# S5 and SwiGLU in parallel on one core: the second x chunk and the parameters on GpSimd's DMA queue, the first weights back to back on SyncE's

## The chip, the core, the metric

The kernel runs on one core of one Trainium2 chip. The metric is device time in microseconds, the median of several executions. Every execution also has a span, from its first to its last instruction; the time is 1.7 to 2.4 us longer than the span.

## The reference

The input x is [2048, 512] in bfloat16. It is normalized (LayerNorm), and two branches read the result: a diagonal complex state space (S5) and a gated feed-forward (SwiGLU). Their sum and x are the output.

```python
xn = _layernorm(x)
# branch A: B_bar from Lambda, log_dt, B;  h_t = Lam_bar * h_(t-1) + B_bar xn_t;  y = 2 Re(C h) + xn * Dskip
# branch B: (silu(xn @ w1) * (xn @ w3)) @ w2        w1, w3: [512, 1792], w2: [1792, 512]
return x + A(xn) + B(xn)
```

## The kernel before

The tokens go in four blocks of four chunks of 128 rows. TensorE is the bottleneck from the first block's gate matmuls on. The change touches only the start, which looks like this (cuts marked with `# ...`). SyncE (`nc.sync`), ScalarE (`nc.scalar`) and GpSimd (`nc.gpsimd`) can issue DMAs.

```python
def load_w(f0, f1, eng1=nc.sync, eng3=nc.sync):       # gate tiles of 128 columns: tile f is f*P .. (f+1)*P
    eng1.dma_start(out=w1_sb[:, :, f0:f1], in_=w1v[:, :, f0:f1])
    eng3.dma_start(out=w3_sb[:, :, f0:f1], in_=w3v[:, :, f0:f1])

for c in range(2):                                     # chunks 0 and 1, each in two halves on two queues
    for eng, dsl in ((nc.sync, slice(0, D // 2)), (nc.scalar, slice(D // 2, D))):
        eng.dma_start(out=x_blk[0][:, c, dsl], in_=xv[:, c, dsl])
nc.scalar.dma_start(out=x_blk[0][:, 3, :], in_=xv[:, 3, :])
nc.sync.dma_start(out=x_blk[0][:, 2, :], in_=xv[:, 2, :])
load_w(0, 2 * P)
for i, src in enumerate((A_log_dt, A_Lambda_re, A_Lambda_im)):     # the parameters, 1 KB each
    nc.sync.dma_start(out=par_rows[i * NPT:(i + 1) * NPT, :], in_=src.rearrange("(t p) -> t p", p=P))
load_w(2 * P, 4 * P)
# ... later loads of x blocks 1, 2, 3 on nc.sync, each as one DMA: load_x(1), load_x(2), load_x(3)

keep_busy(NWARM, TBLK)                                 # NWARM = 10 warm-up matmuls on TensorE
# ...
ln_stats(0, 0)              # VectorE, program order: statistics of chunk 0,
ln_first_rstd(0)            # (ScalarE)
bulk_loads()
ln_stats(0, 1)              # then of chunk 1,
ln_first_rstd(1)
ln_first_transpose(0, 2)    # and only then the normalization of chunk 0, which TensorE transposes
keep_busy(4, P)
ln_apply(0, 1)
ln_first_transpose(1)
# ... statistics and normalization of chunks 2 and 3
quarter(0, (0, 1), 2)       # TensorE: chunk 0 times gate tiles 0 and 1 (w1, then w3)
pps = params_transpose()    # TensorE transposes the parameters; ScalarE and GpSimd go on with them
params_dt(pps)
params_turn()
table_angles(0)             # VectorE, from the parameters
table_angles(1)
quarter(1, (0, 1))
ln_first_transpose(2)
quarter(0, (2,))            # chunk 0 times gate tile 2
ln_first_transpose(3)
# ...
```

## Time and profile before

| | |
|---|---|
| time | 204.51 us, median of 3 (204.32 to 204.80) |
| span of the profiled execution | 203.1 us |
| TensorE busy | 198.3 us (98%) |
| end of TensorE's part of the chain that ended last | 198.87 us (its very last matmul ends at 200.08) |

The view of waits of the kernel before, for TensorE alone, has two lines: who waited for whom, the sum in us, how often, the longest. The second is the launch; the first is the only time in 203 us that TensorE waited for data.

```profile
PE bu_ps L557 <- DMA w_sb<-in_B_w_dram: 1.0, 1, 1.0
PE bu_ps L193 <- PEq L883: 0.8, 1, 0.8
```

The timeline of the kernel before, TensorE alone: start, duration, engine, line of the kernel, operation, output and input, count, and in brackets the idle time before it with what ended it. L193 is the warm-up, L238 the transposes of x, L557 the quarters, L525 the full gate matmuls.

```profile
0.76 4.43 PE L193 MATMUL bu_ps<-const-bfloat16-1.0 128*128 128x512 bf16 x10 [0.76 <-PEq L883]
5.10 0.65 PE L238 MATMUL y_ps<-ident,xn 128*128 128x128 bf16 x4
...
8.49 0.39 PE L557 MATMUL bu_ps<-xnT,w_sb 128*128 128x128 bf16 x4
9.89 0.40 PE L557 MATMUL bu_ps<-xnT,w_sb 128*128 128x128 bf16 x4 [1.01 <-DMA w_sb<-in_B_w_dram]
...
13.47 8.80 PE L525 MATMUL gu_ps<-xnT,w_sb 128*128 128x512 bf16 x40
```

TensorE comes out of its warm-up at 5.19 us straight into the transposes. At 8.49 us it multiplies with the w1 half of gate tile 2; the w3 half is not there until 9.89. The view of the chain that ended last says the same: a DMA of weights, and from 9.89 us on TensorE without a hole.

```profile
4.71 5.13 DMA w_sb<-in_B_w_dram
9.85 0.05 issue
9.89 0.40 PE bu_ps L557 x4
```

And VectorE, in the timeline of all engines, waits for chunk 1 (the second of the statistics), but only for 0.17 us:

```profile
2.82 0.69 DVE L214 BATCH_NORM_STATS2 stats<-x_blk 128x6 f32<-128x512 bf16 x1 [2.82 <-DMA x_blk<-in_A_x_dram]
3.90 0.69 DVE L214 BATCH_NORM_STATS2 stats<-x_blk 128x6 f32<-128x512 bf16 x1 [0.17 <-DMA x_blk<-in_A_x_dram]
```

The trace also records when each of the 16 DMA engines signs off a transfer. "First..last" below is the first and the last of the 16.

```
kernel before, profiled execution       issued   landed, first..last engine
x chunk 1, two halves                    1.16    2.89..3.69 and 3.12..3.88
gate tiles 0/1, w1 and w3           2.11, 2.59   5.11..5.47 and 5.90..6.48
gate tiles 2/3, w1                       4.27    6.80..7.79
gate tiles 2/3, w3                       4.71    7.60..9.85
```

### The profile page before, as it was taken

What the parts mean: (1) busy time and instruction counts of PE and PEld (TensorE: products, weight loads), DVE (VectorE), ACT (ScalarE), POOL (GpSimd) and SP (SyncE); (2) the same over time, 40 slices, a digit from 0 to 9 for tenths busy, and PEclk for the clock granted to TensorE, in tenths of its full rate; (3) what the DMA queues carried; (4) which work ended last, traced back from release to release, by engine and by line L of the source; (5) the groups of instructions that cost most, each with busy time, mean ns of one, the idle gap of its engine ahead of it and who ended that gap; (6) DMA issues with size and microseconds to landing.
All of it is one profiled execution on the core that took longest, in us unless ns stands there. A gap on an engine that the chain in (4) does not pass through costs nothing.

```text
span 203.1 us, 3444 instructions
## 1 busy us (share of the span) xinstructions
PE 198.3 (98%) x1317; PEld 122.8 (60%) x1317; DVE 172.7 (85%) x242; ACT 125.4 (62%) x251; POOL 39.0 (19%) x65
## 2 busy tenths in 40 slices
PE   8899999999999999999999999999999999999994
PEld 2784444444444488854444445888444458888993
DVE  3779699999999999989949999999999935584832
ACT  4699897699999977959766676110566662101010
POOL 3250269700310143021111010310101110000000
PEclk9999999999999999999999999999999999999999
DMA  6899999992573042926796004466330780101011
GB/s 173 248 247 191 312 203 106 350 281 42 101 146 66 0 90 57 183 86 118 68 194 131 13 13 94 91 143 132 90 65 0 149 162 2 52 3 52 29 40 39
DMA packets 28696, 23.16 MB, mean 114 GB/s; under 512 B 16008, under 2 KB 26376, under 8 KB 28680
## 3 DMA queue, kind: packets, MB, share of 16 engines
q1 hardware_dynamic: 25512, 13.21, 27.9%
q0 software_dynamic: 2592, 9.44, 24.9%
q10 hardware_dynamic: 576, 0.30, 0.5%
q8 instruction: 10, 0.16, 0.3%
q14 instruction: 6, 0.05, 0.1%
HBM read 7.74 MB, written 2.10 MB: 48 GB/s over the span
## 4 chain that ended last, share of the span: by engine, by line
PE 93%; DMA 3%; SPq 2%; DVE 1%; issue 0%
PE gu_ps L525 45%; PE gu_ps L724 16%; PE y_ps L724 9%; PE bu_ps L724 7%; PE bu_ps L435 7%; PE y_ps L435 7%; DMA w_sb<-in_B_w_dram 3%; PE gu_ps L557 1%; PE bu_ps L557 1%; DVE xn L735 1%; SPq L166 0%; SPq L151 0%; SPq L161 0%; SPq L152 0%; DVE x_blk L735 0%
## 5 line engine op out<-in xcount | busy, mean ns | idle before, releaser
L525 PE MATMUL gu_ps<-xnT,w_sb 128*128 128x512 bf16 x424 | 92.5, 379 | 0.0
L525 PEld LDWEIGHTS <-w_sb 128*128 128x128 bf16 x424 | 41.4, 98 | 49.4
L724 PEld LDWEIGHTS <-act 128*128 128x128 f16 x451 | 43.2, 98 | 5.5
L534 ACT ACTIVATE g<-gu_ps 128x512 bf16<-128x512 f32 x55 | 33.1, 602 | 14.6 <-PE gu_ps L525 14.4
L535 ACT ACTIVATE u<-gu_ps 128x512 bf16<-128x512 f32 x55 | 33.2, 603 | 9.8 <-PE gu_ps L525 9.5
L543 DVE TENSOR_TENSOR act<-g,u 128x1024 f16<-128x1024 bf16 x28 | 19.0, 677 | 4.4 <-ACT u L535 4.4
L435 PEld LDWEIGHTS <-bt 128*128 128x128 bf16 x128 | 12.5, 98 | 15.1
L478 DVE TENSOR_TENSOR_SCAN u<-rho,act,u 128x512 bf16<-128x512 f32 x16 | 19.6, 1266 | 0.0
L492 POOL DMA_DIRECT2D act<-p x8 | 7.2, 900 | 45.8 <-DVE act L488 31.8
L435 PE MATMUL bu_ps<-xnT,bt 128*128 128x512 bf16 x64 | 15.1, 379 | 0.0
L435 PE MATMUL y_ps<-xnT,bt 128*128 128x512 bf16 x64 | 15.1, 379 | 0.0
L457 DVE TENSOR_TENSOR p<-u,tabe 128x2048 bf16<-128x2048 bf16 x8 | 9.8, 1219 | 2.6 <-DMA act<-p 2.5
L724 PE MATMUL y_ps<-tw,act 128*128 128x256 f16 x88 | 10.9, 272 | 0.0
L437 ACT ACTIVATE u<-y_ps 128x512 bf16<-128x512 f32 x16 | 9.5, 595 | 2.3 <-PE y_ps L435 2.1
L724 PE MATMUL gu_ps<-w_sb,act 128*128 128x256 bf16 (+1 forms) x84 | 10.8, 268 | 0.0
L724 PE MATMUL gu_ps<-tw,act 128*128 128x256 f16 x88 | 10.7, 273 | 0.0
L437 ACT ACTIVATE u<-bu_ps 128x512 bf16<-128x512 f32 x16 | 9.5, 595 | 2.0 <-PE bu_ps L435 1.9
L468 POOL DMA_DIRECT2D u<-p x6 | 5.3, 878 | 26.8 <-ACT u L535 7.9
L744 ACT ACTIVATE bu_ps<-y_ps 128x256 f32<-128x256 f32 x4 | 1.5, 369 | 13.7 <-PE y_ps L724 13.7
L461 DVE TENSOR_TENSOR u<-u,tabe 128x2048 bf16<-128x2048 bf16 x8 | 9.8, 1220 | 0.2
L478 DVE TENSOR_TENSOR_SCAN u<-rho,ends,u 128x512 bf16<-128x512 f32 x8 | 9.9, 1268 | 0.0
L484 DVE TENSOR_TENSOR p<-u,tabe 128x2048 f16<-128x2048 bf16 x8 | 9.8, 1221 | 0.1
(143 smaller groups left out, 275.1 us busy)
## 6 DMA issues: line engine op xcount, KB each, us to landing
act<-p POOLq DMA_DIRECT2D x8, 512.0 KB, 4.7
u<-p POOLq DMA_DIRECT2D x6, 512.0 KB, 4.7
xn<-x_blk POOLq DMA_DIRECT2D x4, 512.0 KB, 5.6
out_dram<-xn SPq DMA_DIRECT2D x15, 128.0 KB, 1.7
w_sb<-in_B_w_dram SPq DMA_DIRECT2D x1, 1792.0 KB
x_blk<-in_A_x_dram SPq DMA_DIRECT2D x3, 512.0 KB, 9.0
w_sb<-in_B_w_dram SPq DMA_DIRECT2D x2, 768.0 KB, 7.1
w_sb<-in_B_w_dram SPq DMA_DIRECT2D x4, 256.0 KB, 3.7
```

The source lines that it names most:

```text
L435: nc.tensor.matmul(out=ps, lhsT=bt[:, ri, dt, pt * P:(pt + 1) * P], rhs=xnT_blk[b][:, dt, :], start=(dt == 0), stop=(dt == NDT - 1))
L437: nc.scalar.activation(out=u[:, j, ri, :], in_=ps, func=ACT.Copy)
L457: nc.vector.tensor_tensor(out=st["p"][:, :, ::-1, :], in0=st["g"], in1=tabe[:, psl, 2:0:-1, :], op=ALU.mult)
L461: nc.vector.tensor_tensor(out=st["g"], in0=st["g"], in1=tabe[:, psl, 0:1, :].to_broadcast(FULL), op=ALU.mult)
L478: nc.vector.tensor_tensor_scan(out=v, data0=rho[:, pt:pt + 1].to_broadcast([P, TBLK]), data1=v, initial=init, op0=ALU.mult, op1=ALU.add)
L484: nc.vector.tensor_tensor(out=st["p16"][:, :, ::-1, :], in0=st["g"], in1=tabe[:, psl, 1:3, :], op=ALU.mult)
L492: gp.dma_start(out=act_state(b, hf), in_=st["p16"], accum_op=ALU.add)
L525: nc.tensor.matmul(out=ps[:, tsl], lhsT=w[:, dt, f * P:(f + 1) * P], rhs=xnT[:, dt, tsl], start=(dt == 0), stop=(dt == NDT - 1))
L534: nc.scalar.activation(out=g16[:, f % 2, :], in_=g_ps, func=ACT.Silu)
L535: nc.scalar.activation(out=u16[:, f % 2, :], in_=u_ps, func=ACT.Copy)
L543: nc.vector.tensor_tensor(out=act(b)[:, k0:k1 + 1:k1 - k0, :], in0=g16, in1=u16, op=ALU.mult)
L724: nc.tensor.matmul(out=out, lhsT=left[:, k, :], rhs=right[k][:, cols], start=(start and k == 0), stop=(k == NK - 1), skip_group_check=True)
```

## The change

The intent: take everything out of SyncE's queue that stands ahead of the weights of gate tiles 2 and 3, so that they are issued some 1.6 us earlier and TensorE's one stall goes. (Landing is the moment at which a transfer's data are in and its semaphore has been counted up.) Chunk 1 and the parameters go to GpSimd's queue; the parameters' transpose moves behind the next quarter; and later loads of x are split.

```diff
-    for c in range(2):
-        for eng, dsl in ((nc.sync, slice(0, D // 2)), (nc.scalar, slice(D // 2, D))):
-            eng.dma_start(out=x_blk[0][:, c, dsl], in_=xv[:, c, dsl])
+    nc.gpsimd.dma_start(out=x_blk[0][:, 1, :], in_=xv[:, 1, :])
+    for eng, dsl in ((nc.sync, slice(0, D // 2)), (nc.scalar, slice(D // 2, D))):
+        eng.dma_start(out=x_blk[0][:, 0, dsl], in_=xv[:, 0, dsl])
     # ... chunks 3 and 2
     load_w(0, 2 * P)
-    for i, src in enumerate((A_log_dt, A_Lambda_re, A_Lambda_im)):
-        nc.sync.dma_start(out=par_rows[...], in_=...)
     load_w(2 * P, 4 * P)
     # ...
-        load_x(1)
+        load_x(1, 2)
     # ...
-        load_x(2)
-        load_x(3)
+        load_x(2, 4)
+        load_x(3, 2)
     # ... after the memset and affine_select of ident on GpSimd
+    for i, src in enumerate((A_log_dt, A_Lambda_re, A_Lambda_im)):
+        nc.gpsimd.dma_start(out=par_rows[...], in_=...)
     # ...
             quarter(0, (0, 1), 2)
+            quarter(1, (0, 1))
             pps = params_transpose()
     # ... params_dt, params_turn, table_angles(0), table_angles(1)
-            quarter(1, (0, 1))
             ln_first_transpose(2)
```

More of the change, by code (lines that the diff above doesn't have):

```diff
@@ L164 @@
     load_w(0, 2 * P)
-    for i, src in enumerate((A_log_dt, A_Lambda_re, A_Lambda_im)):
-        nc.sync.dma_start(out=par_rows[i * NPT:(i + 1) * NPT, :], in_=src.rearrange("(t p) -> t p", p=P))
     load_w(2 * P, 4 * P)
@@ L200 @@
                             base=0, pattern=[[-1, P]], channel_multiplier=1)
+    for i, src in enumerate((A_log_dt, A_Lambda_re, A_Lambda_im)):
+        nc.gpsimd.dma_start(out=par_rows[i * NPT:(i + 1) * NPT, :], in_=src.rearrange("(t p) -> t p", p=P))
     nc.gpsimd.iota(iota_i, pattern=[[1, TBLK]], base=1, channel_multiplier=0)
```

## The prediction

> **What bounds the kernel now.** TensorE: busy 198.3 of 203.1 us (page, part 1). The chain of waits runs through TensorE without a gap from 9.89 us to 198.87 us. So only the start can move the total. TensorE's only data stall there is at 9.89: the third gate tile's first w3 matmul waited 1.0 us (the waits view says 1.01) for the w3 columns of tiles 2 and 3. In the landing records that load was issued at 4.71 and landed engine by engine from 7.60 to 9.85; its w1 twin was issued at 4.27 and landed at 7.79. Before the stall, TensorE is dense from 5.10 (it comes out of its warm-up matmuls, which end at 5.19) to 8.88.
>
> **What the change removes, adds, moves.**
> - SyncE issues at 0.40 to 0.51 us each. The three parameter issues (0.44, 0.26, 0.29) and one half-chunk issue (0.41) leave its queue ahead of the weights. Tiles 2 and 3 should be issued near 2.6 and 3.1 instead of 4.27 and 4.71.
> - The parameters' packets leave the weights' rings. The DMA rate per 25 ns shows a trough at 5.55 to 6.2 us (some 300 GB/s down to 130) just where they pass, and the spread of the 16 engines' landings grows after it: 0.6 us (tile 0/1 w3), 1.0, 2.25 (the stalled load).
> - Bytes are unchanged: 1.57 MB of x and tile 0 to 3 weights. The Trainium skill ("DMA: Bandwidth & Descriptors", Issuing engines are not separate DMA queues) says another issuing engine saves only issue time; the trace agrees in that DMA runs near 300 GB/s whenever fed. From a first packet at 1.75, an estimate with those 300 GB/s puts the stalled load's landing at 7.6 to 8.6, before TensorE wants it (8.66 after its w1 half).
> - x chunk 1 comes over GpSimd. Later GpSimd DMAs took 0.86 us to issue and 0.57 us more to the first packet; from 0.72 that makes landing about 3.2 to 3.9 against 3.88 now. VectorE's second statistics (3.90, ahead of the first normalization) wait for it.
> - GpSimd's three parameter issues (some 0.9 us each) put its iota and cast 2.7 to 3.6 us later, finished near 6.5, wanted at 9.1: free. Parameters land near 7, and their transpose now stands behind quarter 1: no TensorE wait. VectorE's angle tables start about 0.6 us later (9.7), still done before the first gate product.
> - Split loads of x blocks 1 to 3: seven issues instead of three, off the chain.
>
> **On the critical path.** Up to 1.0 us, the whole stall, if chunk 1 is not later than today. ScalarE's table load (11.26) follows TensorE and moves along. VectorE is full from 25 to 82 us and moves only some 0.6 us, but the tightest operand I see (the s4 difference, done 75.46, read 76.46) has 1.0 us of slack. I count 0.8 us.
>
> **Prediction: 203.7 us, 80% range 203.0 to 205.0.** Faster by over 2%: 0.01; within 2%: 0.98; slower: 0.01.
>
> **Right if** the waits view shows no TensorE wait on weights (or under 0.3 us), the chain becomes dense from about 5.1 us, the first tile-3 matmul group (13.64 now) starts near 12.7, and everything later keeps that offset.
>
> **Wrong if** GpSimd's first DMA has a cold start: the first one in this trace sent its first packet 3.74 us after its issue ended, all later ones within 0.8. VectorE was in long bf16 products then, so the cause is open (the skill, "SBUF — State Buffer", The "DVE blocks DMA" trap, would fit; at 0.7 us VectorE is idle). With it chunk 1 lands near 6, normalization slips 2 us and the result is about 205.5. Also wrong if the straggling DMA engines stay 2 us behind without the parameters, or if VectorE's smaller shift makes TensorE wait near 76 us.

## The result, and the profile after

| | before | after |
|---|---|---|
| time, median of 4 | 204.43 us (204.32 to 204.80) | 204.29 us (204.16 to 204.34) |
| ratio | | 0.9989, 95% interval 0.9972 to 1.0006: the same |
| span of the profiled execution | 203.1 us | 202.4 us |

Ratios are the mean time of one kernel's fast runs over that of the other's in the same rounds, so they are not quite the ratio of the medians.

The two profiles differ by 0.7 us, the times by 0.14 us. That is the first thing to notice: the profile before was taken in an execution (204.89 us) longer than each of the four that were timed.

The view of waits of the kernel after, TensorE alone. The wait for weights is gone and a wait for VectorE's normalization is new:

```profile
PE bu_ps L191 <- PEq L883: 0.8, 1, 0.8
PE y_ps L238 <- DVE xn L219: 0.6, 1, 0.6
```

The timeline of the kernel after, TensorE alone. The first transposes stand at 5.80 instead of 5.10 us; there is no gap at gate tile 2 (x8 at 9.04), and the full gate matmuls start 0.63 us earlier than in the profile before (12.84 for 13.47).

```profile
5.80 0.54 PE L238 MATMUL y_ps<-ident,xn 128*128 128x128 bf16 x4 [0.61 <-DVE xn L219]
...
8.81 0.40 PE L238 MATMUL y_ps<-ident,xn 128*128 128x128 bf16 x4
9.04 0.61 PE L557 MATMUL bu_ps<-xnT,w_sb 128*128 128x128 bf16 x8
```

Those full matmuls, and chunk 1's path, are in the timeline of all engines: GpSimd's DMA instruction starts at 1.27 us, VectorE's second statistics wait 0.73 us for the chunk and start at 4.60 instead of 3.90.

```profile
1.27 0.74 POOL L159 DMA_DIRECT2D x_blk<-in_A_x_dram  x1 [0.84 <-POOLq L883]
...
4.60 0.69 DVE L214 BATCH_NORM_STATS2 stats<-x_blk 128x6 f32<-128x512 bf16 x1 [0.73 <-DMA x_blk<-in_A_x_dram]
...
12.84 3.40 PE L525 MATMUL gu_ps<-xnT,w_sb 128*128 128x512 bf16 x14
```

The chain that ended last, kernel after, now begins with chunk 1 instead of the weights, 3.31 us from GpSimd's issue to the landing:

```profile
1.27 3.31 DMA x_blk<-in_A_x_dram
4.58 0.02 issue
4.60 0.70 DVE stats L214
```

The landing records:

```
kernel after, profiled execution        issued   landed, first..last engine
x chunk 2 / chunk 3 (SyncE, ScalarE) 1.18, 1.16  3.19..3.79 / 3.38..3.97
x chunk 1 (GpSimd; first packet 3.12)    1.27    3.94..4.58
gate tiles 0/1, w1 and w3           1.64, 2.11   4.80..5.71 and 5.72..6.57
gate tiles 2/3, w1                       2.67    6.60..7.46
gate tiles 2/3, w3                       3.21    7.47..8.32
```

So the weights did what was hoped, 9.85 to 8.32 us, and chunk 1 took part of it back. The stall cost 1.19 us in that profile: the eight matmuls of gate tile 2 began at 8.49 and ended at 10.29, and without a gap they take 0.61 us, as in the kernel after, and would have ended at 9.10. (The expectations below count 1.35 us.) The late chunk 1 put the first transposes 0.70 us back; at gate tile 2 TensorE is still 0.55 us behind (9.04 for 8.49). That leaves 0.64 us, which is about the difference of the two profiles. Three questions remain: why the times do not show those 0.65 us, what chunk 1 costs, and what the split loads do.

### The profile page after: what moved, and what is told of

Read it like the earlier page. It is cut to its first block, busy times and chain, and to the rows that moved or that the text cites. A ratio compares the mean times of both kernels' runs of the same rounds, so it can differ in the third digit from the quotient of the medians.

```text
span 202.4 us, 3438 instructions
## 1 busy us (share of the span) xinstructions
PE 197.4 (98%) x1304; PEld 122.5 (61%) x1317; DVE 172.5 (85%) x242; ACT 125.1 (62%) x251; POOL 44.7 (22%) x69
## 4 chain that ended last, share of the span: by engine, by line
PE 95%; DMA 2%; DVE 1%; issue 1%; POOLq 0%
PE gu_ps L525 45%; PE gu_ps L724 16%; PE y_ps L724 9%; PE bu_ps L724 7%; PE y_ps L435 7%; PE bu_ps L435 7%; PE gu_ps L557 2%; DMA x_blk<-in_A_x_dram 2%; PE bu_ps L557 1%; PE y_ps L238 1%; DVE xn L735 1%; DVE stats L214 0%; DVE x_blk L735 0%; DVE xn L219 0%; PE bu_ps L191 0%
```

## The experiments

Twelve runs on three chips, four on each, every one with five timed rounds beside the kernel before on the same chip. The table has spans of all executions (us): lowest, median, highest. The chips are numbered here as they come up; on which chip the first result was taken is not on record here.

```
chip  run              lowest  median  highest   before there: lowest, median, highest   ratio (95% interval)
1     before_again     202.0   202.1   202.2     201.9  202.1  203.3                     0.9988 (0.9968 to 1.0007)
1     x1_hw            202.3   202.75  202.8                                             1.0020 (0.9999 to 1.0041)
1     x3_gp            202.3   202.5   204.3                                             1.0019 (0.9987 to 1.0051)
1     par_only         203.0   203.45  203.7                                             1.0049 (1.0026 to 1.0073)
2     after_again      202.4   202.8   204.9     202.1  202.6  203.0                     1.0039 (1.0003 to 1.0074)
2     x1_hw_turned     202.1   202.6   203.2                                             1.0004 (0.9986 to 1.0021)
2     x1_only_turned   202.4   202.65  203.9                                             1.0013 (0.9992 to 1.0034)
2     splits_only      202.3   203.0   203.2                                             1.0024 (1.0008 to 1.0041)
3     par_turned       202.1   202.2   202.7     201.9  202.3  203.3                     0.9995 (0.9967 to 1.0024)
3     par_behind       202.9   203.35  204.2                                             1.0051 (1.0025 to 1.0077)
3     after_warm8      202.3   203.9   205.0                                             1.0070 (1.0033 to 1.0108)
3     after_warm12     202.5   202.6   202.7                                             1.0006 (0.9983 to 1.0029)
```

All gave correct outputs. The main theory at first (A) was: the stall is a steady 1.35 us and the late chunk 1 takes half of it back. The rivals: the stall was a slow draw (B), or the gain is lost later in the kernel (C).

### before_again: is the stall always there?

No edit.

> The kernel before, unchanged, to see another draw of its profile; the first one fell in the longest of its four executions (204.80 us against 204.32 to 204.51). Theory A (the stall on the tile 2/3 w3 weights is a steady 1.35 us, from 8.94 where the same work would have ended to 10.29): the load again lands near 9.8 us and TensorE waits about 1.0 us for it; time 204.4. Rival B (the first profile caught a slow draw of a straggling DMA engine): the load lands near 9.4 us, the wait is 0.5 to 0.7 us, the span is some 0.4 us shorter than 203.1.

TensorE's waits in this profile of the unchanged kernel before: the line with the weights is missing.

```profile
PE bu_ps L193 <- PEq L883: 0.8, 1, 0.8
```

Its timeline, TensorE alone: the gate tile 2 matmuls are one group of eight, and the full gate matmuls start at 12.45, a whole us earlier than in the first profile.

```profile
8.44 0.82 PE L557 MATMUL bu_ps<-xnT,w_sb 128*128 128x128 bf16 x8
...
12.45 8.80 PE L525 MATMUL gu_ps<-xnT,w_sb 128*128 128x512 bf16 x39
```

The tile 2/3 w3 load was issued even later than the first time (5.15 for 4.71 us) and landed at 7.87..8.82. So what made 9.85 us of it in the first profile was not the issue but one of the 16 DMA engines that fell behind: fifteen had signed off by 8.58, the last at 9.85. Span 202.0; all six executions lie between 202.0 and 202.2, and the other eleven on that chip between 201.9 and 203.3, with three over 202.5. Theory A is out, and B holds more strongly than it was stated. The stall is not quite gone: the first w3 matmul of gate tile 2 starts 0.26 us after the matmul before it, where neighbours start 0.056 us apart, so about 0.2 us against 1.18 counted the same way in the first profile. The view of waits doesn't list so short a gap. How often an execution is slow differs: on chip 2 six of the eleven of the kernel before lie at 202.6 or over, and in the first result its four timed executions began at 204.32, where the lowest on the three chips are 203.74 to 204.01. What the slow executions without a profile lost is not shown. Measured against this undisturbed execution, the kernel after (12.84 for 12.45) starts its full matmuls 0.39 us later, and keeps that to the end: matched weight load by weight load, the offset is 0.39 us at every point from 9 to 199 us. Its first transposes are 0.72 us later (5.80 for 5.08), so it does gain 0.33 us in between, the short stall included, and loses more.

### after_again: both kernels on one chip

No edit.

> The changed kernel, unchanged, beside the kernel before on one chip, to set both against the undisturbed execution of the kernel before that the last call showed (span 202.0, no wait for weights). Theory D: the changed kernel has no weight stall in any execution but a fixed 0.4 us later start (chunk 1 at 4.6 us), so its spans lie at 202.3 to 202.5; the kernel before lies at 201.9 to 202.3 in most executions and at 202.6 to 203.3 in the few in which a DMA engine straggles. Ratio 1.001 to 1.002 here. Theory A (a steady stall in the kernel before) would give 0.997 or less.

The lowest span is 202.4, the undisturbed one of the kernel before there 202.1; the median 202.8 against 202.6. That is near the fixed cost of theory D; the profiled execution (202.8) is 0.78 us behind the undisturbed kernel before, twice as much. The ratio, 1.0039, is worse than expected, because two of the six executions are at 204.3 and 204.9, which no disturbed execution of the kernel before reaches. They are taken up below. In this profile chunk 1 landed at 4.97 us, its last engine 0.39 us after the others, and the tile 2/3 w3 load at 8.48, again with no wait for weights.

### x1_hw and x1_hw_turned: chunk 1 back on the fast queues

```diff
 # x1_hw, against the kernel after
-    nc.gpsimd.dma_start(out=x_blk[0][:, 1, :], in_=xv[:, 1, :])
-    for eng, dsl in (...):                    # chunk 0 in halves
+    for c in range(2):
+        for eng, dsl in (...):                # chunks 0 and 1 in halves
 # x1_hw_turned: the same, and load_x(1) and load_x(3) whole again, load_x(2, 4) stays
```

> The changed kernel, with x chunk 1 back in two halves on SyncE's and ScalarE's queues. Theory A (chunk 1 landing at 4.58 instead of 3.88 us puts TensorE's start 0.70 us later and takes back that much of the gain): TensorE's first transpose is back at 5.10 us, the first matmul group of gate tile 3 starts near 12.3 to 12.5 instead of 13.00, and the time falls by 0.5 to 0.7 us to about 203.7. Rival C (what the start gains is lost later, on VectorE or on the loads): the start moves as in A but the time stays within 0.2 us of the changed kernel's 204.29. Under the rival that weights bound the start whatever chunk 1 does, TensorE starts at 5.10 but waits again for the weights and the time stays near 204.2.

> Chunk 1 in halves on SyncE and ScalarE, parameters on GpSimd, and only the load of x block 2 split, so that the count of SyncE and ScalarE DMAs ahead of the last stores is that of the kernel before (3 taken away, 3 added). Theory E (the last stores take their completion semaphores in rotation among eight, and the closing waits go through the eight in a fixed order, so a rotation turned by two costs 0.38 us at the end): the time from TensorE's last weight load to the end is 3.14 us again instead of 3.52, and the time falls by 0.4 us against the run with all loads split, to 204.1 to 204.2. Rival: the late weights of gate tiles 0 and 1 (7.18 us) are all that was slow there; then the tail stays at 3.5 us and the time near 204.5.

TensorE starts at 5.05 and 5.06 us in the two, as theory A had it, but the time did not fall: 204.59 us. Two things are in the profile of x1_hw. The weights of gate tiles 0 and 1 landed at 7.18 us and TensorE waited for them (0.2 us in the view of waits; the quarter's second half starts at 7.22):

```profile
PE gu_ps L557 <- DMA w_sb<-in_B_w_dram: 0.2, 1, 0.2
```

And the end is longer, 3.52 us from TensorE's last weight load to the end instead of 3.14.

The end is where the split loads come in. The trace shows that SyncE's and ScalarE's DMAs take eight completion semaphores in turn, and that SyncE closes the program by waiting for all eight in a fixed order, one wait every 0.06 us. The times below are from the trace (number of the semaphore in brackets):

```
              last three stores landed                    closing waits of SyncE that come after
before        201.75 [106]  201.97 [107]  202.14 [109]    201.76 [106]  201.99 [107]  202.16 [109]
x1_hw         201.12 [109]  201.34 [100]  201.51 [102]    201.36 [100]  201.53 [102]  201.59 [103]  201.65 [104]
                                                          201.71 [105]  201.77 [106]  201.83 [107]  201.89 [109]
```

In the kernel before, the last store has the last semaphore of the order: when it lands, everything else has been waited for. x1_hw has three DMAs fewer (parameters) and five more (splits), so the turn is two further on, the last store has the second semaphore, and six waits are still to come when it lands: 0.36 us. The kernel after has five fewer (three parameters, two halves of chunk 1) and five more: turn unchanged, tail 3.14 us. With the count restored, x1_hw_turned has a tail of 3.16 us, as theory E expected. Its time (204.43 us) is that of the kernel before (204.44), not the 204.1 to 204.2 that was expected: in the median it is 0.2 us under the kernel after on that chip (204.66), and no gain on the kernel before. The profile fell in the longest of the six executions, in which TensorE also waited 0.6 us for a transposing DMA (xnT) later on.

### par_only and par_turned: the parameters alone

```diff
 # par_only, against the kernel before: the three parameter loads from nc.sync to nc.gpsimd, behind affine_select
 # par_turned: the same, and
-        load_x(2)
+        load_x(2, 4)
```

> The kernel before with only the parameters moved to GpSimd's queue; chunk 1, the order of the quarters and the whole loads stay. Theory A: this part is the whole gain; the tile 2/3 w3 load lands at 8.2 to 8.5 us, no wait on weights, TensorE starts at 5.10, time about 203.7. Rival (the later loads' split or the moved quarter matters): TensorE waits for the parameters' transpose near 7.3 us, as they land at 8.5 over GpSimd and the old order wants them at 7.26; then up to 1.2 us of wait and no gain, time 204.3 to 204.9.

> The kernel before with the parameters on GpSimd's queue and the load of x block 2 in four parts, so that the turn of the completion semaphores is that of the kernel before (3 taken away, 3 added). Theory E: the tail is 3.14 us again instead of 4.40, the start is as in the run without the added parts (about 0.25 us later than an undisturbed kernel before), spans 202.0 to 202.6, where the run without the parts had 203.0 to 203.7. Rival (the parameters on GpSimd delay the end in some other way): spans stay over 203.

par_only lost 1.3 us in the median, and 0.9 us in the best of its six executions against the kernel before's median. In its profile TensorE is only 0.25 us behind the undisturbed kernel before (it waited 0.4 us for weights of tiles 0 and 1, landed at 7.06, while the old order of the parameters' transpose cost nothing: they landed at 5.01 to 6.90). The rest is the tail, 4.40 us. par_turned, three loads more, has a tail of 3.15 us and the time of the kernel before (ratio 0.9995). So the parameters on GpSimd alone bring nothing. In the profile of par_turned the stall itself is back, as the tile 2/3 w3 load landed at 7.66..9.14 us:

```profile
PE bu_ps L557 <- DMA w_sb<-in_B_w_dram: 0.4, 1, 0.4
```

And the split of a load of which TensorE never waits is worth a whole us to it. The turn does not explain all of that us: see the next run.

### splits_only: the turn by itself

```diff
 # against the kernel before
-        load_x(1)      ...  load_x(2)      ...  load_x(3)
+        load_x(1, 2)   ...  load_x(2, 4)   ...  load_x(3, 2)
```

> The kernel before with nothing but the loads of x blocks 1, 2 and 3 in 2, 4 and 2 parts: five DMAs more, the rotation turned by five as in the run with the parameters alone on GpSimd (three fewer, the same turn in eight). Theory E: start and middle as in the kernel before, but a tail of about 4.4 us instead of 3.14, time 1.0 to 1.3 us above the kernel before. Rival (the splits are free and the parameters on GpSimd caused that run's loss): tail 3.14, time as the kernel before.

The tail is 3.36 us: the last store took semaphore 105 and three closing waits followed its landing, some 0.2 us. The expected 4.40 was wrong. So the turn alone accounts for 0.06 to 0.07 us per wait that is left. What par_only has beyond that is in its last stores: SyncE issued the second last half store 0.4 us late (200.08 us, where ScalarE's was issued at 199.66), and the two landed at 202.37 and 202.18, 0.9 and 1.2 us after their first engine, where other kernels' take 0.2. In both stores fifteen of the 16 engines signed off within 0.2 us (by 201.65 and 201.16) and one came 0.7 and 1.0 us later. Why SyncE issued late, and why all six executions are long, stays open; there is one profile. The profile of splits_only also shows the kernel before's stall once more, as the tile 2/3 weights landed at 9.02 and 9.77 us:

```profile
PE bu_ps L557 <- DMA w_sb<-in_B_w_dram: 0.8, 2, 0.4
```

### x1_only_turned and x3_gp: chunk 1 alone, and another chunk in its place

```diff
 # x1_only_turned, against the kernel before: chunk 1 whole on nc.gpsimd; load_x(1, 2) and load_x(3, 2) keep the turn
 # x3_gp, against the kernel after
-    nc.gpsimd.dma_start(out=x_blk[0][:, 1, :], in_=xv[:, 1, :])
+    nc.gpsimd.dma_start(out=x_blk[0][:, 3, :], in_=xv[:, 3, :])
-    nc.scalar.dma_start(out=x_blk[0][:, 3, :], in_=xv[:, 3, :])
+    nc.scalar.dma_start(out=x_blk[0][:, 1, :], in_=xv[:, 1, :])
```

> The kernel before with chunk 1 alone on GpSimd's queue, and the loads of x blocks 1 and 3 in two parts so that the count is kept (2 taken away, 2 added). Theory: chunk 1 lands near 4.6 us, TensorE's first transpose moves from 5.08 to 5.7 or 5.8, the tail is 3.14 us, and every span is 0.4 to 0.7 us over the undisturbed 202.0 of the kernel before: 202.4 to 202.7, time about 204.4. With the start 0.7 us later the weights (8.8 us) are there when wanted, so no stall either. If the changed kernel's fixed cost came from the parameters on GpSimd instead, this run is at 202.0 to 202.1.

> The changed kernel with chunks 1 and 3 exchanged: chunk 3, needed last, comes over GpSimd's queue, chunk 1 whole over ScalarE's. Theory A: chunk 1 lands near 3.9 us as chunk 3 did there, TensorE starts at 5.1 to 5.2, chunk 3 lands near 4.6 before VectorE's fourth statistics (about 6.6) want it, and the time is that of the kernel with chunk 1 in halves, about 203.7, or 0.5 to 0.7 us less than the changed kernel. If instead any load on GpSimd's queue costs the start, it stays near 204.2.

x1_only_turned came out as expected: chunk 1 at 4.69 us, first transposes at 5.91, lowest span 202.4. So chunk 1 alone is enough for the fixed cost of the kernel after; par_turned, with the parameters alone, has spans from 202.1 beside 201.9 of the kernel before there.

x3_gp failed as an improvement: its lowest span, 202.3, is not below the kernel after's. Chunk 1, whole on ScalarE's queue, landed at 3.58..4.87 us in its profile, together with chunk 2 (4.66) and chunk 3 (5.13). So leaving GpSimd's queue did not bring chunk 1 in on time. A shared rate would explain it. In the kernel before, the two halves of chunk 1 come straight behind chunk 0, and chunks 2 and 3 are issued 0.46 us after them. In x3_gp and in the kernel after, three chunks of 128 KB on three queues go through at once. An estimate from the measured 248 to 302 GB/s in the stretch from 2.0 to 4.0 us of the kernel after: 384 KB take 1.3 to 1.6 us, 128 KB take 0.4 to 0.5; chunk 0 is in at 2.9, so chunk 1 is in at 3.4 if it comes alone, and at 4.2 to 4.5 if it shares. The Trainium skill says the same of queues in general ("DMA: Bandwidth & Descriptors", Issuing engines are not separate DMA queues): DMAs of all issuing engines interleave on the same 16 DMA engines, and only issue time is saved. The landings agree with it but do not show it. In the kernel after, chunk 3 had the place in ScalarE's queue that chunk 1 has here and landed at 3.38..3.97, before chunk 1; and the profile of x3_gp has late engines (14 of 16 had signed off chunk 1 by 4.32, the last two at 4.70 and 4.87). How much is sharing and how much late engines stays open.

The profile of x3_gp was taken in its one slow execution (span 204.3), and that points to what slows executions of after_again too. Its timeline, TensorE alone:

```profile
0.76 4.43 PE L191 MATMUL bu_ps<-const-bfloat16-1.0 128*128 128x512 bf16 x10 [0.76 <-PEq L883]
6.09 0.65 PE L238 MATMUL y_ps<-ident,xn 128*128 128x128 bf16 x4 [0.90 <-DVE xn L219]
...
7.38 3.25 PE L557 MATMUL gu_ps<-xnT,w_sb 128*128 128x128 bf16 x32
```

The same 32 matmuls in the timeline of the kernel after:

```profile
6.82 1.95 PE L557 MATMUL gu_ps<-xnT,w_sb 128*128 128x128 bf16 x32
```

3.25 against 1.95 us. In x3_gp successive 128-column matmuls start 0.107 us apart until 10.0 us; in the kernel after 0.056 us from 6.1 us on. The page's clock row shows nines from its first slice and so hides it: the trace has no clock record before 10.10 us, and the views count such time as full. The records have the full clock from 10.10 us on in x3_gp and from 5.83 in the kernel after; in the other profiles it begins anywhere from 4.01 to 6.39 us. The Trainium skill ("TensorE: Matmul & The Clock Gate", Part 1: The HAM clock gate) describes a clock that is halved until a free-running window of about 3.4 us was busy, 106.7 ns a matmul of 128 columns before and 55.6 after; both rates agree with the trace. 10.10 less 3.41 (the page's window, so this is an estimate) is 6.69: theory F is that in this execution a window ended at 6.69 us, had the idle 0.90 us before 6.09 in it, and did not count as busy, so that the next one, ending at 10.10, had to do. The other profiles fit, laid out the same way: the window that ends where the full clock begins has at most 0.71 us of idle TensorE (after_warm8; 0.61 in the kernel after), the one before it always 0.90 or more.

### after_warm8 and after_warm12: idle time before the first transpose, more and less

```diff
 # against the kernel after
-    NWARM = 10
+    NWARM = 8          # after_warm12: 12
```

> The changed kernel with 8 warm-up matmuls in place of 10: the warm-up ends near 4.3 us, and with the first transpose at 5.8 to 6.2 TensorE stands idle for 1.5 to 1.9 us. Theory F (the rare executions at 203.9 to 204.9 of the kernels with a late chunk 1 are those in which the idle time falls into the stretch that decides on TensorE's full clock, which then [...]costs 1.3 us or more): far more of the six executions are slow, three or more at 203.5 or over. Rival (those executions are straggling DMA engines): no more than one of six.

> The changed kernel with 12 warm-up matmuls: they end near 5.9 us, so hardly any idle time before the first transpose. Theory F: no execution at 203.5 or over; spans 202.4 to 202.9, about the changed kernel's usual ones or 0.1 to 0.2 above. Rival: as often slow as the changed kernel, one or two of six.

With 8 warm-up matmuls five of six executions have spans of 203.8 to 205.0 us; the sixth (202.3) is the profiled one, where the full clock came at 5.04 us in spite of an idle 1.4 us:

```profile
PE y_ps L238 <- DVE xn L219: 1.4, 1, 1.4
```

With 12 none of six is over 202.7. With 10 and a late chunk 1 (the kernel after, x3_gp, x1_only_turned) 4 of 22 are at 203.9 or over; with 10 and chunk 1 on time, none of the 33 of the kernel before. That is what theory F says, and not what straggling DMA engines would do. Two things limit it. The late full clock was caught in one profile only (x3_gp). For the two slow executions of after_again the record has the granted clock, 0.992 and 0.991, the lowest of all executions (the others have 0.997 or more). That is some 3.3 and 3.7 us at half clock in the records (an estimate: twice 0.8% and 0.9% of their spans), where 0.997 is 1.2 us. So the clock is at work there too, but these records differ from x3_gp's, whose slow start stands in none (1.0), and there is no profile to tell where in the execution it was. For the slow ones of after_warm8 and x1_only_turned (1.0, as in x3_gp) a late full clock is inferred. And par_behind, with chunk 1 on time, has two executions at 204.0 and 204.2, 1.1 us over its lowest, which theory F does not explain. after_warm12 does not beat the kernel before: ratio 1.0006.

### par_behind: the same aim without GpSimd

```diff
 # against the kernel before: parameter loads behind load_w(2 * P, 4 * P), still on nc.sync
 # and params_transpose, params_dt, params_turn, table_angles(0), table_angles(1) behind ln_first_transpose(3)
```

> The kernel before with one move: the three parameter loads stay on SyncE's queue, but behind the weights of tiles 2 and 3, and their transpose and the angle tables stand four TensorE steps later. No GpSimd DMA at the start, the count of DMAs unchanged. Theory: TensorE's first transpose at 5.0 to 5.1 us, tile 2/3 w3 issued near 3.6 and landed by 8.3 to 8.7 where no engine straggles, tail 3.14, spans 201.9 to 202.4, with fewer executions over 202.5 than the kernel before; so at or a little under it (ratio 0.998 to 1.000). If the weights' landing is set by the DMA rate alone, it is near 8.8 as in the undisturbed kernel before and the ratio is 1.000.

The start looked the best of all: first transposes at 5.05, weights of tiles 2/3 at 7.48 and 8.26 us, TensorE 0.18 us ahead of the undisturbed kernel before at 9 to 12 us. But the lead was gone by the full gate matmuls, which start at 12.45 in both: the late parameters put ScalarE's table load at 10.50 to 11.79 (10.23 to 11.51 there), ScalarE read the first gate product until 12.40, and TensorE waited for that buffer. And all six executions lie above the kernel before's median. The view of waits of par_behind, TensorE alone:

```profile
PE bu_ps L193 <- PEq L883: 0.8, 1, 0.8
PE bu_ps L724 <- DVE act L766: 0.8, 1, 0.8
```

and its timeline of all engines at that place:

```profile
75.41 0.88 DVE L766 TENSOR_TENSOR act<-act,x_blk 128x1408 f16<-128x1408 f16 x1
...
76.34 0.94 PE L724 MATMUL bu_ps<-w_sb,act 128*128 128x256 bf16 x7 [0.75 <-DVE act L766]
```

This is rival C, found in another kernel than the one it was meant for. VectorE is full from 25 to 82 us, so a delay of its angle tables (10.76 us here, 9.08 in the undisturbed kernel before) is carried 60 us on, to the operand whose slack the prediction gives as 1.0 us (done at 76.29 here). In the kernel after the same operand is done at 75.34 (74.46 and 0.88) and read at 75.82: no wait, half the slack left.

## Why the prediction was right or wrong

Right: the class (within 2%), the range (203.0 to 205.0), no wait for weights, a chain that keeps its offset to the end, the weights' landing (7.6 to 8.6; measured 8.32), the trough in the DMA rate gone, the parameters in time for their moved transpose (at 8.52, not near 7, for a transpose at 8.70), no wait on VectorE at 76 us, and ScalarE's table load moving along (11.26 to 10.62).

Class and range say little for the mechanism: the range is 2 us wide around an expected gain of 0.8 us, and would have held with no gain at all. The times show 0.14 us, with an interval that includes none. Of the prediction's own signs under "Right if", two failed: TensorE was dense from 5.80, not 5.1, and the first tile-3 group started at 13.00, not near 12.7. That the two first profiles differ by 0.7 us, close to the 0.8, is luck: one was a slow draw.

Wrong, by the steps of the prediction:

- "On the critical path. Up to 1.0 us, the whole stall": the sum began from a term that the undisturbed execution does not have. The stall was a slow draw (before_again: 0.2 us; first profile: 1.2). Timed executions at 204.32 to 204.80 beside a profiled one at 204.89 were a warning.
- "if chunk 1 is not later than today", 3.2 to 3.9 us: it landed at 4.58, 4.97 and 4.69 in three profiles. What failed is the first packet, at 3.12 instead of 2.15 (0.72, 0.86 and 0.57). GpSimd's DMA instruction began at 1.27, not at 0.72 where GpSimd's memset had begun (0.55 us), and its first packet came 1.11 us after the instruction's end, not 0.57 (0.54 us); the instruction itself was 0.12 us shorter. From first packet to landing it took 1.46 us, which the prediction's 3.2 to 3.9 allows for (1.05 to 1.75); so this miss needs no shared rate. The feared cold start of 3.74 us did not show.
- "The parameters' packets leave the weights' rings", with less straggling: not borne out. With the parameters on GpSimd the tile 2/3 w3 load still took 0.85 (after), 1.35 (x1_hw_turned) and 1.5 us (par_turned, where TensorE waited for it) from first to last engine. That the parameters add to it is not excluded: the two widest, 2.25 and 2.0 us (splits_only), have them ahead of the weights on SyncE's queue, but so have before_again and x1_only_turned with 0.95 and 1.0. And the load's issue 1.94 us earlier (3.21 for 5.15) bought 0.5 us of landing against the undisturbed kernel before (8.32 for 8.82), so it was not the issue that set it.
- "VectorE's angle tables start about 0.6 us later (9.7)": they started at 10.14, and half of the slack at 76 us went with it.
- "seven issues instead of three, off the chain": eight, in fact (two, four and two), and off the chain only because they put the turn of the completion semaphores back.
- A risk that was not named: an idle TensorE between warm-up and first transposes, which in some executions costs over 1 us; by the matmul spacing of x3_gp it is the clock.

In sum the change trades a stall that is 0.2 us in the undisturbed execution and up to 1.2 us in a slow one for first transposes that come 0.7 us later or more (5.80, 6.19), and for a rare loss of the clock. In the first timing that came out even, on chip 2 a little worse (1.0039). Not tried: to put VectorE's statistics of chunk 1 behind the normalization of chunk 0, so that TensorE's first transposes need not wait for chunk 1.

## What to carry to other kernels

Before costing a stall from one profile, see whether that execution is a usual one: profile the unchanged kernel again, and compare the lowest spans as well as the medians. A second queue saved issue time here (1.6 us for the weights) and brought its own chunk in later; check on the trace when the first packet leaves and what else is under way then. When DMAs are added to or taken from a kernel, look at its last microseconds too, and at the idle time between warm-up and first real work.

## What the Trainium skill lacked or had wrong

- No page tells that the order of the completion semaphores at the end of a program can cost time: closing waits went by at 0.06 us each, and the tail was 3.14, 3.36 or 3.52 us with zero, three or six of them after the last landing.
- "TensorE: Matmul & The Clock Gate" has the run-to-run shift of the window (here the full clock began between 4.01 and 6.39 us) but not that a short idle time in the first busy window can put the full clock off, nor how much idle time a window may have: 0.90 us idle before 6.09 and the full clock at 10.10 us (one profile), 0.71 us idle and the full clock at 5.04 (after_warm8), and five of six executions slow with two warm-up matmuls fewer (their clock was not caught).
- "DMA: Bandwidth & Descriptors", Latency and other measured facts, gives about 1 us to the first byte of a GpSimd DMA. At the start of this kernel it was 1.85 us from the instruction's start and 1.11 from its end; and as GpSimd's first instruction after the launch it began at 1.27 us where a memset began at 0.72, for which we found a reason on no page.
- The same table has DMA engines 7 and 15 as usually slower, and its best guess at the cause is specific to GpSimd's DMAs. In the kernel before no GpSimd DMA is issued until 38.74 us, and still the last of 16 engines landed 2.25 us after the first. The records do not number the engines, so whether they are the ones that the page names is open.
